# Gate and value products of the first network's second half by a seven-product scheme, and half of the second network's weights converted during its first pass

## The chip, the cores and the metric

One NeuronCore of a Trainium2 chip runs the whole program. The metric is the device time of one execution in microseconds (us). The kernel before takes 980.09 us (median of 3 runs, 979.85 to 980.98).

Engines: TensorE (PE, matmuls; its weight loads are PEld), VectorE (DVE), ScalarE (ACT), GpSimd (POOL) and SyncE (SP, which issues nearly all transfers).

## The reference, cut to what matters

Attention over 4 x 8 heads of 576 tokens gives x with 2304 tokens of 512 features. Two feed-forward networks follow:

```python
g = x @ w_gate                      # 512 -> 1536
silu = g * (1.0 / (1.0 + np.exp(-g)))
x = (silu * (x @ w_val)) @ w_out    # 1536 -> 512
h = np.maximum(x @ w_in, 0.0)       # 512 -> 2048
out = h * h @ w_out2                # 2048 -> 512
```

## The kernel before

**Precision.** The weights arrive as 64-bit words and are turned into 32-bit floats on the chip (`bit_stages`, L275: one ScalarE and three VectorE steps on a tile of 128 x 512). Then every operand, weight or activation, is split into a high part (a ScalarE copy, L323, L908, L993) and a low part (a VectorE subtraction, L326, L912, L996). Each product of two operands is three matmuls: high by high, high by low, low by high (`three`, L937 to L940).

**Stages.** Attention comes first, interleaved with the first half of the first network ("B1": 6 chunks of 128 hidden features, then "R" for the tiles that left some out). At about 264 us the attention is done and its buffers are released (`late`, L1181). The second half, "B2" (L1193 to L1204), runs 9 token tiles of 256 tokens over the chunks 6 to 11. Then the second network, "C", runs over 8 weight groups (each two chunks of 128) in two passes.

**A unit of B1 and B2** (`unit_tasks`, L960) is one tile and one chunk: 12 matmuls for the gate, 12 for the value, then tanh (ACT, L974), two VectorE steps (L982, L987), high and low (L993, L996), and 12 matmuls down into banks that collect the output. After a tile's last chunk `add_tasks` (L1055) adds the first half's output, read back into a "ys" buffer, and stores the sum.

**A unit of C** (`c_unit`) is a pair of tiles and a weight group. The four blocks of the up product (two halves of the features, two chunks, two tiles) are made by seven products of 6 matmuls instead of eight, in the order P1, P6, P5, P7, P2, P3, P4; VectorE and ScalarE add the products up between them (L1522, L1525, L1565). The operands are seven blocks or differences of blocks per pair (`x_pair`, L1358), in the "xs" buffers; the ninth tile runs alone with four products (`x_single`, L1438). The weights of a group need four combinations on VectorE (`up_task`, L1209, L1239). The first pass runs groups 0 to 3 for pairs 0, 1, 2 and the single tile, then pair 3 runs all eight, then groups 4 to 7 for the rest.

**Weights.** Converted tiles lie in "wg" slots: 18 from the start and 13 more once the attention's buffers are released (`NAMED`, L37). B1's 18 tiles leave theirs as the last tile of B1 uses them (`w_free`). All of C's 8 groups are converted during B2 (L1330 to L1336): groups 2 to 7 are stored to DRAM (`put_by`, L1300) and fetched again later (`fetch`, L1313), groups 0 and 1 stay. Raw weights pass through 4 "wst" buffers and 5 "wf" buffers.

**Order of the work.** The program's order on each engine is made by a list planner (`Order`, L121) that gives every stage a cost (`dve`, `act`, `products`, `dma`) and buffers it must take; units go by a due number, weights by "LATE". Each engine then runs its list in order, waiting by semaphore for what it needs. The planner's costs for VectorE are

```python
    def dve(n, fast=False):
        return 0.067 + n / (1920 if fast else 960)
```

Of the kernel before, what the change touches and what calls it, by code (L numbers as in the profile page):

```python
# [36 lines left out]
NAMED = {"wg": (18, 13), "xs": (4, 5), "wst": (4, 0)}  # L37
N_WST = NAMED["wst"][0]
# [22 lines left out]
def attn_moe_kernel(ctx: ExitStack, tc: tile.TileContext, qT, kT, vw, vin, vp, qp, kp, qs, ks, vs, maskc, masks, identc, wB, wC, out):  # L61
# [60 lines left out]
    class Order:  # L122
        def __init__(self):
            self.flying = []
            self.queues = {k: [] for k in ("x", "qk", "sum", "rows", "v", "att", "w", "mlp", "other", "done", "put")}
            n = {"att": N_ATT, "y": N_Y, "gv": N_GV, "p": N_P, "pt": N_PT, "v": N_V, "xt": N_XT}
            n |= {"wf": N_WF, "sg": N_SG, "hh": N_HH, "ys": 1, "rr": 0, "rh": 0, "rl": 0, "yc": 0}
# [134 lines left out]
    pools = {"wg": [tc.alloc_tile_pool(name="wg1", bufs=1, side="right")], "xs": [com], "wst": [com]}  # L262

    def slot_tile(kind):
        i = order.got[kind].pop(0)
        pool = pools[kind][i >= NAMED[kind][0]]
        shape, dtype = {"wg": ([128, 2, 512], F32R), "xs": ([128, 2, 2, T1], F32R), "wst": ([128, 512, 2], I32)}[kind]
        return i, pool.tile(shape, dtype, tag=f"{kind}{i}", bufs=1, name=kind)
# [3 lines left out]
    def w_give(*keys):  # L272
        return tuple(lambda key=key: ("wg", w_at[key]) for key in keys)
# [34 lines left out]
    def w_task(key, src, due, cond=None):  # L308
# [3 lines left out]
        def load():  # L312
            w_at[key], w_tiles[key] = slot_tile("wg")
            u["hi"], u["lo"] = (w_tiles[key][:, i] for i in range(2))
            u["at"], u["st"] = slot_tile("wst")
            nc.sync.dma_start(out=u["st"], in_=src)
# [5 lines left out]
        def high():  # L322
            nc.scalar.activation(out=u["hi"], in_=u["f"].bitcast(F32), func=AF.Copy)  # L323

        def low():
# [35 lines left out]
    def pool_rows(b, which, half, h):  # L361
        src, dst = (k_t, kd_t) if which == "k" else (q_t, qd_t)
        if b not in dst:

            room = com.tile([128, KD, T1], F32, tag="ys", name="ys").rearrange("p k n -> p (k n)")
# [304 lines left out]
    def global_tasks(b, ins, due, combos, end=False):  # L670
# [5 lines left out]
        def scores():  # L676
# [16 lines left out]
            [Stage("t", cost, scores, ("att", "att", "p", "p"), ("ys",) if end else (), lambda: after(ins + [consts]), 0.92)],  # L693
# [361 lines left out]
    def add_tasks(key, c0, n, dst, y_free):  # L1055
# [3 lines left out]
        def load():  # L1059
            u["y"] = com.tile([128, KD, T1], F32, tag="ys", name="ys")  # L1060
# [14 lines left out]
        def finish(cond, due):  # L1075
# [7 lines left out]
            y_out[key] = Task(adds + [Stage("d", dma(128 * 4 * n), store, (), ("ys",))], due, True)  # L1083
# [25 lines left out]
    def b1_finish(t, tags):  # L1109
# [3 lines left out]
        def make(cond, due):  # L1113
            u = {}

            def copy(i):
                if i == 0:
                    u["y"] = com.tile([128, KD, T1], F32, tag="ys", name="ys")
# [10 lines left out]
            stages.append(Stage("d", dma(128 * 4 * n), store, (), ("ys",)))  # L1129
# [50 lines left out]

    def late():  # L1181
        att.release()
        post = tc.alloc_tile_pool(name="post", bufs=1)
        at = after(sum(att_tasks.values(), sum(x_parts, [])))
        for kind, n in NAMED.items():
            pools[kind].append(post)
# [9 lines left out]
    ya = ("att", "att")  # L1196
# [8 lines left out]
    NFP = NF2 // 4  # L1205
    y2_sp = dram.tile([NTOK // 128, 128, DM], F32, name="y2_sp")
    out_t = out.rearrange("(r p) d -> r p d", p=128)

    def up_task(q, due):  # L1209
# [4 lines left out]
        def load(i):  # L1214
            if i == 0:
                for k in keys:
                    w_at[k], w_tiles[k] = slot_tile("wg")
            u["at", i], u["st", i] = slot_tile("wst")
            for k in (i, i + 2):
                u["f", k] = com.tile([128, 512], I32, tag="wf", bufs=N_WF, name="wf")  # L1220
            nc.sync.dma_start(out=u["st", i], in_=wC[2 * q + i][:, 0])

        def tile_half(i, c):
            return lambda: u["f", i].bitcast(F32)[:, c * 256 : c * 256 + 256]

        def both(k, src, n=512):
            def high():
                nc.scalar.activation(out=w_tiles[keys[k]][:, 0, :n], in_=src()[:, :n], func=AF.Copy)

            def low():  # L1230
                w = w_tiles[keys[k]]
                nc.vector.tensor_tensor(
                    out=w[:, 1, :n], in0=src()[:, :n], in1=w[:, 0, :n].bitcast(F32), op=ALU.subtract
                )

            return high, low

        def combine(o, a, b, op):
            return lambda: nc.vector.tensor_tensor(out=o(), in0=a(), in1=b(), op=op)  # L1239

        def read(i):
            return bit_stages(lambda: u["st", i], lambda: u["f", i], (), lambda: ("wst", u["at", i]))

        a11, a12, a21, a22 = (tile_half(i, c) for i in range(2) for c in range(2))
        s2, s3, s4 = tile_half(2, 0), tile_half(2, 1), tile_half(3, 0)
        high0, low0 = both(0, lambda: u["f", 0].bitcast(F32))
        high1, low1 = both(1, lambda: u["f", 1].bitcast(F32))
        high2, low2 = both(2, lambda: u["f", 2].bitcast(F32))
        high3, low3 = both(3, lambda: u["f", 3].bitcast(F32), 256)
        d = dma(128 * 1024)  # L1250
        second = Task([Stage("d", d, lambda: load(1), ("wst", "wf", "wf"))] + read(1), due, lead=W_LEAD)
        first = Task(
            [Stage("d", d, lambda: load(0), ("wst", "wf", "wf") + ("wg",) * 4, cond=lambda: after([late_]))]
            + read(0)
            + [
                Stage("a", act(512), high0),
                Stage("v", dve(512), low0),
                Stage("v", dve(256), combine(s3, a11, a21, ALU.subtract), cond=lambda: after([second])),
                Stage("v", dve(256), combine(a21, a21, a22, ALU.add)),
                Stage("v", dve(256), combine(s2, a21, a11, ALU.subtract)),  # L1260
                Stage("v", dve(256), combine(s4, a12, s2, ALU.subtract), (), ("wf",)),
                Stage("a", act(512), high1),
                Stage("v", dve(512), low1, (), ("wf",)),
                Stage("a", act(512), high2),
                Stage("v", dve(512), low2, (), ("wf",)),
                Stage("a", act(256), high3),
                Stage("v", dve(256), low3, (), ("wf",)),
            ],
            due,
            lead=W_LEAD,  # L1270
        )
        queues["w"] += [first, second]
        for k in keys:
            w_tasks[k] = first

    kept = {"rr": 2, "rh": 2, "rl": 2, "yc": 2}
    homes = {}

    def keep():
        slots = [(kind, i) for kind in ("wst", "wg") for i in order.got[kind]]  # L1280
        for kind in ("wst", "wg"):
            order.got[kind].clear()
        for kind, n in kept.items():
            homes[kind] = [slots.pop() for _ in range(n)]
            order.free[kind] = [0.0] * n

    def block_tile(name):
        kind, i = homes[name][0]
        homes[name].append(homes[name].pop(0))
        dtype = F32R if name in ("rh", "rl") else F32  # L1290
        pool = pools[kind][i >= NAMED[kind][0]]
        t = pool.tile([128, 2, 512], dtype, tag=f"{kind}{i}", bufs=1, name=name)
        return t if name == "yc" else t.rearrange("p b (c n) -> p (b c) n", c=2)

    w_sp = dram.tile([2 * NFP, 6, 128, 2, 512], F32, name="w_sp")

    def half_of(key):
        return 256 if key[0] == "U" and key[2] == 3 else 512

    def put_by(keys, task):  # L1300
        out_ = []
        for n, key in enumerate(keys):
            at = key[1], (4 + key[2] if key[0] == "D" else key[2])

            def store(key=key, at=at):
                n = half_of(key)
                nc.sync.dma_start(out=w_sp[at][:, :, :n], in_=w_tiles[key][:, :, :n].bitcast(F32))

            out_.append(Task([Stage("d", dma(128 * 1024), store, (), w_give(key), lambda: after([task]))], LATE))
            stored[key] = out_[-1]  # L1310
        queues["put"] += out_

    def fetch(key):  # L1313
# [535 lines left out]
```

## Time and profile before

| | us |
|---|---|
| median of 3 runs | 980.09 |
| the profiled execution | 980.34 |
| its span on the core | 978.6 |
| PE / PEld busy | 968.0 / 907.4 |
| VectorE / ScalarE busy | 668.2 / 385.3 |

The span is the time from the first to the last instruction on the core. Busy time is the union of an engine's records; matmul records are longer than their spacing, since matmuls are pipelined and their ends are modelled, so the spacing is read from their starts. The granted clock ("PEclk") is that of TensorE as a share of 2.4 GHz.

### The profile page before, as it was taken

The numbers are of one execution on the slowest core, as the hardware profiler recorded it, in microseconds if no ns is written. First come the engines' busy times: TensorE is split into PE (matmuls) and PEld (weight loads), VectorE is DVE, ScalarE is ACT, GpSimd is POOL, SyncE is SP. The second block draws the span as 40 slices with busy tenths as digits, with TensorE's granted clock in tenths as the row PEclk, the third lists the DMA queues.
The fourth block names the chain that finished last, engine by engine and source line by source line (L and its number), as shares of the span: only waits on it lengthen the run. The fifth ranks groups of instructions, "written<-read, shape, count | busy, mean of one in ns | idle before, by whom it ended". The sixth has DMA issues, their size and how long they took to land.

```text
span 978.6 us, 20467 instructions
## 1 busy us (share of the span) xinstructions
PE 968.0 (99%) x8397; PEld 907.4 (93%) x8397; DVE 668.2 (68%) x1500; ACT 385.3 (39%) x926; POOL 24.2 (2%) x31
## 2 busy tenths in 40 slices
PE   9989999999999999999999999999999999999998
PEld 7878999999999999999999999889889889898897
DVE  6998978469589488888898346647455437584643
ACT  4576464354455355454444222324233113232221
POOL 0202011000000000000000000000000000000000
PEclk9998999999999999999999999999999999999999
DMA  9989868051565257877892264113024802140202
GB/s 289 280 264 218 228 156 187 12 160 43 164 216 172 72 174 246 266 257 269 288 302 76 66 237 151 44 44 108 1 86 140 280 12 79 51 130 22 87 1 86
DMA packets 90874, 145.93 MB, mean 149 GB/s; under 512 B 21149, under 2 KB 60061, under 8 KB 90781
## 3 DMA queue, kind: packets, MB, share of 16 engines
q1 hardware_dynamic: 87324, 136.66, 42.6%
q0 software_dynamic: 3456, 7.96, 4.8%
q8 instruction: 66, 1.08, 0.4%
q14 instruction: 28, 0.22, 0.1%
HBM read 103.71 MB, written 40.89 MB: 148 GB/s over the span
## 4 chain that ended last, share of the span: by engine, by line
PE 97%; DVE 1%; ACT 1%; issue 0%; DVEq 0%; ACTq 0%
PE gv L938 14%; PE gv L940 13%; PE gv L939 13%; PE y L938 7%; PE y L940 7%; PE y L939 7%; PE att L1634 7%; PE att L1635 7%; PE att L1636 7%; PE att L542 2%; PE att L600 2%; PE y L1143 2%; PE att L690 2%; PE att L939 2%; PE att L938 1%; PE att L940 1%
## 5 line engine op out<-in xcount | busy, mean ns | idle before, releaser
L938 PE MATMUL gv<-xs,wg 128*128 128x256 f32 x1120 | 318.0, 284 | 0.0
L939 PE MATMUL gv<-xs,wg 128*128 128x256 f32 x1120 | 314.9, 281 | 0.0
L940 PE MATMUL gv<-xs,wg 128*128 128x256 f32 x1120 | 314.9, 281 | 0.0
L938 PEld LDWEIGHTS gv<-xs,wg 128*128 128x128 f32 x1120 | 212.3, 190 | 3.3 <-DVE sg L987 0.2
L939 PEld LDWEIGHTS gv<-xs,wg 128*128 128x128 f32 x1120 | 212.4, 190 | 2.0
L940 PEld LDWEIGHTS gv<-xs,wg 128*128 128x128 f32 x1120 | 212.3, 190 | 0.0
L1634 PE MATMUL att<-wg,rh 128*128 128x512 f32 x288 | 113.7, 395 | 0.0
L1635 PE MATMUL att<-wg,rh 128*128 128x512 f32 x288 | 113.5, 394 | 0.0
L1636 PE MATMUL att<-wg,rl 128*128 128x512 f32 x288 | 113.2, 393 | 0.0
L1525 DVE TENSOR_TENSOR rr<-y,ss 128x256 f32<-128x256 f32 x96 | 40.4, 421 | 94.2 <-PE y L940 94.1
L993 ACT ACTIVATE hh<-sg 128x256 fp32r<-128x256 f32 x108 | 44.8, 415 | 118.0 <-DVE sg L987 113.5
L938 PE MATMUL y<-hh,wg 128*128 128x256 f32 x312 | 90.9, 291 | 0.0
L1606 ACT ACTIVATE rh<-rr 128x512 fp32r<-128x512 f32 (+1 forms) x80 | 46.8, 588 | 108.0 <-DVE rr L1599 107.5
L939 PE MATMUL y<-hh,wg 128*128 128x256 f32 x312 | 88.6, 284 | 0.0
L940 PE MATMUL y<-hh,wg 128*128 128x256 f32 x312 | 88.5, 284 | 0.0
L987 DVE SCALAR_TENSOR_TENSOR sg<-sg,gv 128x256 f32<-128x256 f32 x108 | 45.2, 418 | 56.7 <-PE gv L940 55.5
L982 DVE SCALAR_TENSOR_TENSOR sg<-sg,gv 128x256 f32<-128x256 f32 x108 | 45.1, 418 | 39.6 <-ACT sg L974 39.2
L940 PE MATMUL y<-xs,wg 128*128 128x256 f32 x256 | 72.0, 281 | 0.0
L939 PE MATMUL y<-xs,wg 128*128 128x256 f32 x256 | 71.9, 281 | 0.0
L938 PE MATMUL y<-xs,wg 128*128 128x256 f32 x256 | 71.9, 281 | 0.0
L974 ACT ACTIVATE sg<-gv 128x256 f32<-128x256 f32 x108 | 41.4, 384 | 74.1 <-PE gv L940 71.7
L1636 PEld LDWEIGHTS att<-wg,rl 128*128 128x128 f32 x288 | 54.1, 188 | 12.8 <-DVE rl L1609 0.2
(110 smaller groups left out, 1762.3 us busy)
## 6 DMA issues: line engine op xcount, KB each, us to landing
wst<-wB SPq DMA_DIRECT2D x36, 512.0 KB, 6.8
wst<-wC SPq DMA_DIRECT2D x32, 512.0 KB, 5.9
w_sp<-wg SPq DMA_DIRECT2D x30, 512.0 KB, 10.0
wg<-w_sp SPq DMA_DIRECT2D x30, 512.0 KB, 4.7
y_sp<-ys SPq DMA_DIRECT2D x20, 512.0 KB, 3.5
xt<-y_sp SPq DMA_DIRECT2D x16, 512.0 KB, 3.8
xt<-x_sp SPq DMA_DIRECT2D x11, 512.0 KB, 4.7
ys<-y_sp SPq DMA_DIRECT2D x11, 512.0 KB, 4.7
```

The costliest lines, as they stand in the source:

```text
L938: nc.tensor.matmul(o, w[:, 0], x[:, 0], start=start, stop=False, skip_group_check=more)
L939: nc.tensor.matmul(o, w[:, 0], x[:, 1], start=False, stop=False, skip_group_check=more)
L940: nc.tensor.matmul(o, w[:, 1], x[:, 0], start=False, stop=stop, skip_group_check=more)
L974: nc.scalar.activation(out=u["s"], in_=u["g"][:, :n], func=AF.Tanh, scale=0.5)
L982: nc.vector.scalar_tensor_tensor(out=u["s"], in0=u["s"], scalar=1.0, in1=u["g"][:, :n], op0=ALU.add, op1=ALU.mult)
L987: nc.vector.scalar_tensor_tensor(out=u["s"], in0=u["s"], scalar=0.5, in1=u["v"][:, :n], op0=ALU.mult, op1=ALU.mult)
L993: nc.scalar.activation(out=u["h"][:, 0], in_=u["s"], func=AF.Copy)
L1525: return lambda: nc.vector.tensor_tensor(out=o(), in0=u[ps][:, :T1], in1=a(), op=ALU.add)
L1606: nc.scalar.activation(out=u["h"][:, b0:b1], in_=r(b0, b1), func=AF.Copy)
L1634: nc.tensor.matmul(o, h[:, c], w[:, 0], start=first and i == 0, stop=False)
L1635: nc.tensor.matmul(o, h[:, c], w[:, 1], start=False, stop=False)
L1636: nc.tensor.matmul(o, l[:, c], w[:, 0], start=False, stop=last and i == 1)
```

## The change

B2 is done by pairs of tiles, like C: the gate chunk and the value chunk take the place of the two chunks of a group, so seven products of 6 matmuls give gate and value of both tiles. The tiles are visited as pair 0, the ninth tile alone (four products), pairs 1, 2, 3. VectorE adds the products up (five additions and one ScalarE copy in a unit), then each tile has the steps tanh, silu, times, high, low and its down product as before, with sums in new "ss" and "h2" buffers. The gate and value weights of a chunk go through `up_task` and leave three "wg" tiles and one half-size "wh" tile. There are 6 extra "wg" slots instead of 13, and 6 "wh" slots; a tile takes its slot only when its high part is made, not when its raw data are loaded. When the first network's weights are done, two "wst" buffers become one more "wg" slot and a second "ys" buffer. Of C's groups, 2 and 3, then 0 and 1, are converted during B2; groups 4 to 7 are converted and stored during C's first pass, two "wg" slots then serving as raw buffers. Each converted tile is stored as soon as it is ready, where a group's four up tiles were stored together.

The diff, cut to its core:

```diff
-NAMED = {"wg": (18, 13), "xs": (4, 5), "wst": (4, 0)}
+NAMED = {"wg": (18, 6), "wh": (0, 6), "xs": (4, 5), "wst": (4, 0), "ss": (0, 8), "h2": (0, 4), "ys": (1, 0)}
...
-                Stage("d", dma(128 * 1024), load, ("wst", "wg"), cond=cond),
+                Stage("d", dma(128 * 1024), load, ("wst",) + ("wg",) * early, cond=cond),
...
-                Stage("a", act(512), high),
+                Stage("a", act(512), high, ("wg",) * (not early)),
...
-    for j in range(NF, NF1):
-        for i in range(3):
-            w_task((j, i), wB[j][:, i], LATE, lambda: after([late_]))
...
-    for t in range(NT1):
-        x_task(("B2", t), T1, lambda t=t: load_x(x_sp, t), lambda t=t: after([spills[t]]), ("xt",))
-        tags = ya if t % 2 == 0 else y2
-        early, finish = add_tasks(("B2", t), t * T1, T1, y_sp, tags)
-        for j in range(NF, NF1):
-            unit_tasks("B2", t, j, T1, j == NF, j == NF1 - 1, tags, finish, t == NT1 - 1, early)
...
+        put(0, 0, 512, ())
+        stages.append(combine(s3, a11, a21, ALU.subtract, ("wf",), lambda: after([second])))
+        stages.append(combine(a21, a21, a22, ALU.add))
+        put(1, 1, 512, ())
+        stages.append(combine(a11, a21, a11, ALU.subtract))
+        stages.append(combine(a12, a12, a11, ALU.subtract))
+        stages[-1].give = ("wf",)
+        put(2, 0, 512, ("wf",))
+        put(3, 2, 256, ("wf",))
...
+    for j in range(NF, NF1):
+        convert(("f", j), [wB[j][:, i] for i in range(2)], {(j, 2): wB[j][:, 2]})
+
+    def spare():
+        a, b = order.got["wst"]
+        order.got["wst"].clear()
+        alias["wg", SPARE_WG], alias["ys", 1] = ("wst", a), ("wst", b)
+        order.named["wg"].append((0.0, SPARE_WG))
+        order.named["ys"].append((0.0, 1))
...
+    def b2_unit(g, j, spent):
...
+            pe("P1", "x1", "A11", "B11", True, True, ("gv",))
+            pe("P6", "x2", "S2", "T2", True, True, ("gv",))
+            pe("P5", "z", "S1", "T1", True, True, ("y",))
+            pe("P7", "y", "S3", "T3", True, True, ("y",))
+            pe("P2", "x1", "A12", "B21", False, True, (), [lambda: at(mid, 0)()])
+            pe("P3", "z", "S4", "B22", False, True, (), [lambda: at(mid, 2)()])
+            pe("P4", "y", "A22", "T4", False, True, (), [lambda: at(mid, 3)()])
+            mid = Task(
+                [
+                    Stage("a", act(T1, True), begin, ("ss",), (), lambda: after([steps["P1"]])),
+                    Stage("v", d, add("s", "x2", "s"), (), ("gv",), lambda: after([steps["P6"]])),
+                    Stage("v", d, add("r", "z", "s", True), ("ss",), (), lambda: after([steps["P5"]])),
+                    Stage("v", d, add("r", "y", "r"), (), (), lambda: after([steps["P7"]])),
+                    Stage("v", d, add("g", "z", "s", True), ("ss",), ("y",), lambda: after([steps["P3"]])),
+                    Stage("v", d, add("s", "y", "s"), (), ("y",), lambda: after([steps["P4"]])),
+                ],
+                due - 1.5,
+                True,
+            )
...
+    visits = [0, NPAIRS, *range(1, NPAIRS)]
+    for g in visits:
+        whole = [spills[t] for t in range(2 * g, min(2 * g + 2, NT1))]
+        (x_single if g == NPAIRS else x_pair)(("B2", g), g, n_unit[0] + 0.5, x_sp, whole)
+        for j in range(NF, NF1):
+            b2_unit(g, j, g == visits[-1])
...
-    for q in range(KEEP_AT, 2 * NFP):
-        convert(q)
-        put_by([("U", q, i) for i in range(4)], w_tasks["U", q, 0])
-        for i in range(2):
-            put_by([("D", q, i)], w_tasks["D", q, i])
-    for q in range(KEEP_AT):
-        convert(q)
...
+    for q in range(KEEP_AT, NFP):
+        convert_c(q)
+        put_by(keys_of(q))
+    for q in range(KEEP_AT):
+        convert_c(q)
...
+    for q in range(KEEP_AT, NFP):
+        for key in keys_of(q):
+            fetch(key)
+    queues["w"].append(Task([Stage(None, 0.0, raw, ("wg",) * 2, cond=lambda: after([keep_b_]))], LATE))
+    for q in range(NFP, 2 * NFP):
+        convert_c(q)
+        put_by(keys_of(q))
+    for q in range(NFP, 2 * NFP):
+        for key in keys_of(q):
+            fetch(key)
```

## Rows read from the trace of the kernel before

**Rows 1.** The page: span, and busy time of each engine, share and instructions.
```profile
span 978.6 us, 20467 instructions
PE 968.0 (99%) x8397; PEld 907.4 (93%) x8397; DVE 668.2 (68%) x1500; ACT 385.3 (39%) x926; POOL 24.2 (2%) x31
```

**Rows 2.** Waits of PE, whole span: line, releaser, total us, times, longest us.
```profile
PE y L1143 <- ACT zeros L1137: 2.3, 1, 2.3
PE att L709 <- DVE xt L618: 1.2, 1, 1.2
...
PE att L600 <- ACT p L459: 0.2, 1, 0.2
```

**Rows 3.** The page: the chain that ended last, by engine.
```profile
PE 97%; DVE 1%; ACT 1%; issue 0%; DVEq 0%; ACTq 0%
```

**Rows 4.** Timeline of SP: output stores of B1's and B2's last tiles, first pass's last.
```profile
364.14 0.56 SPq L1123 DMA_DIRECT2D y_sp<-ys  x1
...
594.71 0.56 SPq L1068 DMA_DIRECT2D y_sp<-ys  x1
...
743.57 0.36 SPq L1703 DMA_DIRECT2D y_sp<-yc  x1
```

**Rows 5.** Timeline of PE in B2: first and last of 67 matmuls in a row.
```profile
364.00 0.28 PE L938 MATMUL att<-hh,wg 128*128 128x256 f32 x1
...
371.92 0.28 PE L938 MATMUL gv<-xs,wg 128*128 128x256 f32 x1
```

**Rows 6.** Stretches: length, busy of PE, PEld, DVE, ACT, POOL; PEclk, DMA share, GB/s.
```profile
338.00:364.00 26.00, 26.00 (x224) 26.00 (x223) 21.75 (x46) 14.91 (x31) 0.00 (x0) 1.00 0.61 201
...
494.00:519.00 25.00, 25.00 (x212) 25.00 (x211) 23.25 (x50) 11.87 (x25) 0.00 (x0) 1.00 0.87 294
...
543.00:570.00 27.00, 27.00 (x229) 27.00 (x228) 9.68 (x23) 6.78 (x16) 0.00 (x0) 1.00 0.23 71
...
364.00:595.00 231.00, 231.00 (x1936) 230.66 (x1935) 174.51 (x377) 93.86 (x204) 0.00 (x0) 1.00 0.64 219
```

**Rows 7.** Timeline of PE in C: first of 24 products, and the one after them.
```profile
850.09 0.28 PE L938 MATMUL y<-xs,wg 128*128 128x256 f32 x1
...
852.94 0.28 PE L938 MATMUL y<-xs,wg 128*128 128x256 f32 x1
```

**Rows 8.** Timeline of DVE in B2, operations back to back.
```profile
455.48 0.42 DVE L982 SCALAR_TENSOR_TENSOR sg<-sg,gv 128x256 f32<-128x256 f32 x1
455.81 0.69 DVE L297 SCALAR_TENSOR_TENSOR wf<-wst,wf 128x512 int32<-128x512 int32 x1
456.41 0.42 DVE L282 TENSOR_SCALAR wf<-wf 128x512 int32<-128x512 int32 x1
456.74 0.41 DVE L982 SCALAR_TENSOR_TENSOR sg<-sg,gv 128x256 f32<-128x256 f32 x1
```

**Rows 9.** Groups by form: busy us, mean ns | idle before.
```profile
L1525 DVE TENSOR_TENSOR rr<-y,ss 128x256 f32<-128x256 f32 x96 | 40.4, 421 | 94.2 <-PE y L940 94.1
...
L1232 DVE TENSOR_TENSOR wg<-wf,wg 128x512 fp32r<-128x512 f32 x24 | 16.4, 685 | 1.8 <-ACT wg L1228 1.8
...
L1228 ACT ACTIVATE wg<-wf 128x512 fp32r<-128x512 f32 x24 | 15.0, 624 | 9.2 <-DVE wf L297 9.2
...
L1239 DVE TENSOR_TENSOR wf<-wf 128x256 f32<-128x256 f32 x32 | 13.4, 420 | 0.1
...
L1565 ACT ACTIVATE ss<-gv 128x256 f32<-128x256 f32 x32 | 12.0, 374 | 25.2 <-PE gv L940 25.2
```

**Rows 10.** The page: stores of converted weights: count, KB each, median us to landing.
```profile
w_sp<-wg SPq DMA_DIRECT2D x30, 512.0 KB, 10.0
```

**Rows 11.** Stretches, columns as in rows 6: the start, and C's first pass.
```profile
0.00:100.00 100.00, 93.44 (x1201) 80.35 (x1203) 86.38 (x234) 59.78 (x180) 14.70 (x20) 0.95 0.94 263
...
600.00:650.00 50.00, 50.00 (x308) 44.67 (x307) 28.95 (x56) 14.21 (x28) 0.00 (x0) 1.00 0.20 70
```

More of the change, by code (lines that the diff above doesn't have):

```diff
@@ L1246, in up_task @@
[L1246 to L1249, printed above, removed]
-        d = dma(128 * 1024)
[L1251 to L1271, printed above, removed]
@@ L1272, in up_task @@
-        queues["w"] += [first, second]
[L1273 to L1311, printed above, removed]
@@ L1344, in attn_moe_kernel, with put @@
-    UP = {"A11": (0, 0), "A12": (0, 1), "S1": (1, 0), "A22": (1, 1), "S2": (2, 0), "S3": (2, 1), "S4": (3, 0)}
+        s3 = tile_half(2, 0)
+        d = dma(128 * 1024)
+        second = Task([Stage("d", d, lambda: load(1), ("wst",))] + read(1), due, lead=W_LEAD)
+        stages = [Stage("d", d, lambda: load(0), ("wst",), cond=lambda: after([late_]))] + read(0)
+        first = Task(stages, due, lead=W_LEAD)
+        def put(*args):
+            stages.extend(both(*args))
+            w_tasks[keys[args[0]]] = Part(first, len(stages) - 1)
@@ new lines, in attn_moe_kernel @@
+    for j in range(NF, NF1):
[6 more added lines that the diff above has]
+        order.named["ys"].append((0.0, 1))
+    SPARE_WG = sum(NAMED["wg"])
+    queues["w"].append(Task([Stage(None, 0.0, spare, ("wst",) * 2, cond=lambda: after([w_tasks[NF1 - 1, 2]]))], LATE))
@@ L1355, in attn_moe_kernel, with x_pair @@
     PROD = 6 * products(T1)
[L1358 to L1360 removed]
+    def x_pair(key, g, due, src, whole):
         u = {}
@@ L1478, in x_single, with make_pe, pe, go @@
         queues["done"].append(Task([Stage(None, 0.0, lambda: None, (), ("xt",), lambda: after(ends_))]))
+    ya = ("att", "att")
+    def make_pe(u, steps, key, q, due, single, last, free_x, spent):
+        def pe(name, ps, w, x, start, stop, take=(), cond=()):
+            def go():
+                if start:
+                    u[ps] = bank(take[0])
+                product(u[ps], factor(q, w), xh_t[key][x], start, stop, not (start or single))
+            before = list(steps.values())[-1:]
+            def ready():
+                if any(s.at == 0 for s in before):
+                    return None
+                needs = [f() for f in cond] + [after([x_tasks[key][x], w_tasks["U", q, UP[w][0]]])]
+                return None if None in needs else max(needs)
+            give = tuple(lambda x=x: ("xs", x_at[key][x]) for x in free_x.get(name, ()) if last)
+            if spent and name in ("P4", "Q4"):
+                give += w_give(*(("U", q, i) for i in range(4)))
+            steps[name] = Task([Stage("t", PROD, go, take, give, ready)], due + 0.01 * len(steps), True)
+        return pe
@@ new lines, in keys_of, with convert_c, keep_a @@
+    def keys_of(q):
+        return [("U", q, i) for i in range(4)] + [("D", q, i) for i in range(2)]
+    def convert_c(q):
+        convert(q, [wC[2 * q + i][:, 0] for i in range(2)], {("D", q, i): wC[2 * q + i][:, 1] for i in range(2)})
+    stored = {}
+    for q in range(KEEP_AT, NFP):
[3 more added lines that the diff above has]
+        convert_c(q)
+    def keep_a():
+        order.got["ss"].clear()
+        homes["rr"] = [("bk", 0), ("bk", 1)]
+        order.free["rr"] = [0.0] * 2
@@ new lines, in keep_b, with raw @@
+    def keep_b():
+        order.got["h2"].clear()
+        homes["rh"] = [("bk", 2), ("bk", 3)]
+        homes["rl"] = [("wst", i) for i in order.got["wst"]]
+        order.got["wst"].clear()
+        order.free["rh"], order.free["rl"] = [0.0] * 2, [0.0] * 2
+    def raw():
+        for n, i in enumerate(order.got["wg"]):
+            alias["wst", 10 + n] = "wg", i
+            order.named["wst"].append((0.0, 10 + n))
+        order.got["wg"].clear()
+    tails_, downs_b = b2_last
+    direct = [w_tasks[key] for q in range(KEEP_AT) for key in keys_of(q)]
@@ L1493, in c_unit @@
         prev = last_down[0]
-        def pe(name, ps, w, x, start, stop, take=(), cond=()):
-            def go():
-                if start:
-                    u[ps] = bank(take[0])
-                product(u[ps], factor(q, w), xh_t[key][x], start, stop, not (start or single))
-            before = list(steps.values())[-1:]
-            def ready():
-                if any(s.at == 0 for s in before):
-                    return None
-                needs = [f() for f in cond] + [after([x_tasks[key][x], w_tasks["U", q, UP[w][0]]])]
-                return None if None in needs else max(needs)
-            give = ((lambda: ("xs", x_at[key][x])),) * (last and free_x.get(name, False))
-            steps[name] = Task([Stage("t", PROD, go, take, give + w_free_of(name), ready)], due + 0.01 * len(steps), True)
-        def w_free_of(name):
-            return w_give(*(("U", q, i) for i in range(4))) if spent and name in ("P4", "Q4") else ()
+        pe = make_pe(u, steps, key, q, due, single, last, X_ONE if single else X_PAIR, spent)
         def start_r():
@@ L1584, in c_unit @@
             needs = [[at(mid, 4), at(one, 0)], [at(mid, 5)]]
-        if single:
-            steps["Q4"].stages[0].give += ((lambda: ("xs", x_at[key]["B11"])),) * last
-            steps["Q3"].stages[0].give = ()
         def tail(i):
@@ L1674, in c_begin @@
             yc_in[g, h] = Task(
-                [Stage("d", dma(128 * 1024), lambda h=h: load(h), ("yc",), (), lambda n=needs: after(n))], due, True
+                [Stage("d", dma(128 * 1024), lambda h=h: load(h), ("ys",), (), lambda n=needs: after(n))], due, True
             )
```

305 lines of the change are left out of this document (233 added, 72 removed).

## The prediction

> **What bounds the kernel now.** I read the busy table first: TensorE (PE) is busy for 968.0 of 978.6 us [rows 1]. The ends of matmuls are modelled, so a busy PE proves little, and the waits of PE come next: seven in the whole trace, 6.6 us together, the longest 2.3 and 1.2 us, all in the start or the attention lines [rows 2]. The chain that ended last agrees: PE 97% [rows 3]. So the end is set by the number of matmuls times their spacing.
>
> The spacing is read in the changed stage, the first network's second half (B2), from about 364 to 595 us [rows 4]. Matmuls of 256 columns start every 0.12 us without a gap: 66 intervals from 364.00 to 371.92 [rows 5]. Over the stage 1936 fall in 231 us, 0.1193 us each, at a granted clock of 1.00, the 2.4 GHz level [rows 6]. The second network (C) already runs the seven-product scheme: there 24 products start from 850.09 to 852.94, 0.1188 us each, without a gap too [rows 7]. The scheme itself need not starve PE.
>
> The second engine is VectorE (DVE): 23.3 of 25 us at its fullest in B2, 9.7 of 27 after 543 us [rows 6], where the conversion of C's weights has run out. Its records overlap, so I cost an operation from start to start: 0.335 us for 256 columns (455.48 to 455.81) and for the exponent step (456.41 to 456.74), 0.605 for 512 (455.81 to 456.41) [rows 8].
>
> **The matmuls removed.** B2 has 9 token tiles x 6 chunks x 36 matmuls = 1944 (12 gate, 12 value, 12 down). Afterwards a pair of tiles takes 7 products x 6 = 42 for gate and value where 48 stood, and 24 for down as before. Four pairs x 6 chunks are 24 units: 144 matmuls fewer. The ninth tile alone keeps 4 x 6 = 24 and saves nothing. 144 x 0.1193 = 17.2 us, all on PE, which sets the end. The 1008 products that pairs now take, at C's spacing instead of B2's, give 1008 x 0.0005 = 0.5 us more.
>
> [...] The rows show 118 to 120 ns in this stream, and the sum stays with them.
>
> **VectorE, added and moved.** (a) Five additions of products in each pair unit: 120 x 0.335 = 40.2 us. With the six operations of gate times value that both tiles had before, a pair unit needs 11 x 0.335 = 3.7 us beside 66 x 0.1193 = 7.9 us of PE. (b) Operand blocks: a pair needs 7 low parts and 4 differences of 512 columns, the single tile 3 and 1: 48 x 0.605 = 29.0 us where 18 x 0.605 = 10.9 stood, +18.1. (c) A chunk's gate and value weights take two raw reads of 0.335 + 2 x 0.605 = 1.545, four sums of 256 columns, low parts of 3 x 0.605 + 0.335: 6.58; with the down weight's 2.15 it is 8.73. Six chunks: 52.4 where 18 x 2.15 = 38.7 stood, +13.7. (d) A group of C's weights costs 6.58 + 2 x 2.15 = 10.9; four of eight leave B2 for C's first pass, -43.5. Net +28.5 us of VectorE in a stage that gets 17 shorter.
>
> [...]
>
> **Does VectorE still fit?** From the last tile of the first half (338 us) to the end of the new B2 (364 + 214 = 578) are 240 us. In it: that tile's own steps 6.0 + 1.2; B2's units 24 x 3.7 + 6 x 1.0 = 94.4; operand blocks of later visits 22.4, of C's first pair 6.7; nine output additions 10.9; four of C's groups 43.5; and what is left of B2's weights. These need slots: four "wg" per chunk, of which 6 spare ones exist instead of 13 until the last first-half tile frees the other 18. Before that, chunk 6 can run whole (8.7), chunk 7 but for three low parts (7.2), chunk 8's raw reads (3.1): 19.0; 33.4 are left. Sum 218.5, or 91% of 240. Before, PE saw no wait where VectorE was at 93% [rows 2, 6]. So I take the cover as enough on average, and look where it is thinnest.
>
> First pair, from 364 us: of the 33.4, 25.6 - 7.2 = 18.4 fit beside the last first-half tile; 15.0 remain, with 7.9 - 3.7 = 4.2 us per unit for them. The last chunk is due after five units, 39 us, in which 20.8 are free, less 2.4 for the single tile's blocks: it fits with 3 us over. Lower bound of the loss 0; upper, if nothing were converted beside that tile, 33.4 + 18.5 + 2.4 - 39.4 = 14.9 us. I take 0, because the trace shows this conversion running full beside that very tile (21.8 of 26 us) [rows 6].
>
> Entry of C: groups 0 and 1 find slots only as the last pair frees them. Some 5 us of them can run ahead, 16.8 stay for a visit of 47 us that needs 22.2 + 6.7 + 2.4 itself: 15.7 are free, and group 1 is due one C unit later. Groups 2 and 3 go through a single spare slot, 10 tiles x (0.62 high + 0.69 low + 10.0 landing of the store) = 113 us [rows 9, 10], in the 120 from 411 us (first pair done, and with it the first network's weights) to the last visit. Bounds 0 and the 1.1 us lacking plus one chain of high and low; I take 0, since group 1 has 10 us of grace.
>
> Changes of visit (four, and the entry of C): the next operand blocks follow one another out of slots that the last unit frees. C has such changes, with the same 9 slots, and no PE wait is listed there [rows 2]. Bounds 0, or one high and one low part each time, 5 x (0.62 + 0.69) = 6.6 us [rows 9]. I take 1.5, near the row without waits, for B2's last 24 down matmuls cover 2.8 us where C's, of 512 columns, cover twice that.
>
> C's first pass (595 to 744 us [rows 4]): VectorE was at 29 of 50 us [rows 11]; 43.5 more in 148 bring it to 87%, under the 93% above. The transfers that move along, 16 raw tiles and 22 tiles stored of 0.52 MB, 20 MB in all, raise the traffic from 70 to some 200 GB/s, below the 294 that B2 bore [rows 6, 11]. SP issues them in order, ahead of operand loads; what those lose is priced with the changes of visit. ScalarE gains 24 copies of 0.38 us, 13 highs of operands and 6 of weights, about 21 us on 94 of 231 [rows 6]: hidden; without that cover each copy stands between a first and a fifth product. Cost 0.
>
> **Sum.** The profiled execution took 980.3 us (span 978.6, 1.7 around it); the median of the runs is 0.2 lower. 980.3 - 17.2 - 0.5 + 1.5 = 964.1; against the median 963.9.
>
> **Rivals.** One: VectorE takes part of it back. If steps no longer overlap, because each waits for the one before, 0.42 and 0.69 take the place of 0.335 and 0.605 [rows 8], the 218.5 become about 260, 20 over the 240, of which C can take over 10.9: 9 lost, 973; with half of that slip, 968 to 969. For it: 91% load on one queue in order, where a late weight step can stand ahead of an addition that PE awaits. Against: full stretches kept 0.33 and 0.60 [rows 8].
>
> Two: nothing is won. In a unit the fifth to seventh products add to banks that ScalarE or VectorE must have read. If each pair unit waits 0.7 us, an addition and what it queues behind, 24 x 0.7 = 17: 981. Against: C runs the same order without gaps [rows 7].
>
> Three, slower: the first pair starves for weights. The buffers come free only as the last first-half tile ends its gate, value and down products, and raw data has five others; if that holds all 33.4 us of conversion back to 364, 14.9 are lost, near 979. The gaps, some 5 us ahead of each of three units, would then also cost clock: in the first 100 us, where PE has gaps (93.4 busy), 0.95 was granted, later 1.00 [rows 11]. Three units have 198 matmuls; half of them at the 1.2 GHz level are 99 x 0.119 = 11.8 us more: 991. It decides once over 18 us are lost there, which waits alone do not reach. Against: the conversion beside that tile in the trace [rows 6].
>
> That the change does not do what it says is a small chance within the second: seven products are what C already runs.
>
> **Chances.** PE stays the bound, 961 to 967: 0.64. VectorE takes part, 967 to 977: 0.20. Nothing won: 0.06. Starved first pair, slower: 0.10. About 0.2%, 2 us, can be told from no change. Faster 0.64 + 0.20 = 0.84, same 0.06, slower 0.10. The range, 961 to 974, takes in the first case and all of the second but its end: its low end is the sum without the 1.5, less 0.4 for the other 792 matmuls at C's spacing and 1 for the measurement, its high end rival one at full size.
>
> **What would show it.** Right: 8397 - 144 = 8253 matmuls; B2 ending near 578 us at 0.119 us a matmul; PE waits outside attention under 3 us; VectorE near nine tenths from 338 to 578 us and in C's first pass; C still 383 us long. Wrong: waits of PE's product lines for weight or operand lines of VectorE, most of all in the first pair, a granted clock under 1.00 there, or a spacing in B2 above 0.12 us.

## The result, and the profile after

The changed kernel takes 963.82 us (median of 4 runs, 963.13 to 965.32) beside 980.32 for the kernel before; ratio 0.9833, 95% interval 0.9816 to 0.985. Forecast were 963.9 us, range 961 to 974, and faster with a chance of 0.84.

The page of the changed kernel: span, busy time, and the chain that ended last, by engine (compare [rows 1, 3]).

```profile
span 963.5 us, 20487 instructions
PE 950.2 (99%) x8253; PEld 888.9 (92%) x8253; DVE 733.6 (76%) x1686; ACT 406.4 (42%) x975; POOL 23.9 (2%) x31
...
PE 92%; DVE 5%; ACT 1%; issue 1%; DMA 1%; SPq 0%; DVEq 0%; ACTq 0%
```

The 144 matmuls are gone (8397 to 8253). The chain now goes through VectorE for 5% of the span where it was 1%: PE still bounds the kernel, but VectorE has come close.

Its waits of PE: line, releaser, total us, times, longest us (compare [rows 2]). Those outside the start and attention are new.

```profile
PE att L1853 <- DVE rl L1826: 1.1, 1, 1.1
...
PE gv L975 <- DVE sg L1024: 0.6, 1, 0.6
...
PE gv L975 <- DVE ss L1564: 0.4, 1, 0.4
...
PE y L976 <- DVE hh L1033: 0.2, 1, 0.2
```

The timeline of SP after: output stores of a tile near the end of attention, of the last tile of the first half, of pair 0, of B2's last pair, and of the first pass's last tile (compare [rows 4]).

```profile
260.46 0.56 SPq L1161 DMA_DIRECT2D y_sp<-ys  x1
...
365.00 0.52 SPq L1161 DMA_DIRECT2D y_sp<-ys  x1
...
414.14 2.35 SPq L1105 DMA_DIRECT2D y_sp<-ys  x2
...
580.28 2.69 SPq L1105 DMA_DIRECT2D y_sp<-ys  x2
...
728.93 0.36 SPq L1928 DMA_DIRECT2D y_sp<-ys  x1
```

By these stores B2 lasts from 365.0 to 580.3, 215.3 us, where it took 594.7 - 364.1 = 230.6: 15.3 shorter. All before it ends 0.9 later, all after it takes 963.5 - 580.3 = 383.2 instead of 383.9. That makes the 15.1 us between the two spans; the profiled run of the changed kernel was the slowest of its four, so the medians differ by more, 16.5.

The stretches after, by visit (columns as in [rows 6]): the first half's last tile; pair 0; the single tile; pairs 1, 2, 3; the entry of C; and the whole from 338 to 578 us.

```profile
338.00:364.00 26.00, 25.22 (x210) 24.81 (x210) 25.68 (x57) 17.54 (x38) 0.00 (x0) 1.00 0.43 130
364.00:410.00 46.00, 45.60 (x385) 45.39 (x385) 45.34 (x113) 22.40 (x51) 0.00 (x0) 1.00 0.37 122
410.00:436.00 26.00, 26.00 (x222) 25.99 (x221) 21.94 (x46) 10.77 (x24) 0.00 (x0) 1.00 0.65 223
436.00:483.00 47.00, 47.00 (x400) 47.00 (x399) 41.18 (x101) 20.02 (x46) 0.00 (x0) 1.00 0.43 147
483.00:530.00 47.00, 47.00 (x400) 47.00 (x400) 37.56 (x90) 16.81 (x40) 0.00 (x0) 1.00 0.34 109
530.00:577.00 47.00, 47.00 (x400) 47.00 (x399) 46.11 (x112) 23.56 (x53) 0.00 (x0) 1.00 0.62 217
577.00:620.00 43.00, 41.87 (x278) 38.12 (x277) 40.12 (x81) 18.73 (x36) 0.00 (x0) 1.00 0.56 190
...
338.00:578.00 240.00, 238.82 (x2015) 238.20 (x2015) 218.82 (x516) 111.50 (x251) 0.00 (x0) 1.00 0.47 156
```

PE is idle for 26.00 - 25.22 = 0.8 us, then 0.4, then 43.00 - 41.87 = 1.1 at the entry of C: 2.3 in all, and for nothing between. VectorE is busy for 218.8 of 240 us, with 71.0 of 72 from 338 to 410 us and 46.1 of 47 in the last visit. These are the places to test.

### The profile page after: what moved, and what is told of

The parts are those of the page before. It is cut to its first block, busy times and chain, and to the rows that moved or that the text cites. A ratio compares the mean times of both kernels' runs of the same rounds, so it can differ in the third digit from the quotient of the medians.

```text
span 963.5 us, 20487 instructions
## 1 busy us (share of the span) xinstructions
PE 950.2 (99%) x8253; PEld 888.9 (92%) x8253; DVE 733.6 (76%) x1686; ACT 406.4 (42%) x975; POOL 23.9 (2%) x31
## 4 chain that ended last, share of the span: by engine, by line
PE 92%; DVE 5%; ACT 1%; issue 1%; DMA 1%; SPq 0%; DVEq 0%; ACTq 0%
PE gv L975 11%; PE gv L977 10%; PE gv L976 10%; PE y L975 8%; PE y L976 8%; PE y L977 8%; PE att L1851 7%; PE att L1853 7%; PE att L1852 7%; PE att L976 2%; PE att L977 2%; PE att L975 2%; PE att L579 2%; PE att L637 2%; PE att L727 2%; PE y L1181 1%
## 5 line engine op out<-in xcount | busy, mean ns | idle before, releaser
L975 PE MATMUL gv<-xs,wg 128*128 128x256 f32 x880 | 250.1, 284 | 1.0 <-DVE sg L1024 0.6
L977 PE MATMUL gv<-xs,wg 128*128 128x256 f32 x880 | 246.9, 281 | 0.0
L976 PE MATMUL gv<-xs,wg 128*128 128x256 f32 x880 | 246.8, 280 | 0.0
L975 PEld LDWEIGHTS gv<-xs,wg 128*128 128x128 f32 x880 | 166.0, 189 | 4.6 <-DVE sg L1024 1.0
L976 PEld LDWEIGHTS gv<-xs,wg 128*128 128x128 f32 x880 | 166.0, 189 | 1.9
L977 PEld LDWEIGHTS gv<-xs,wg 128*128 128x128 f32 x880 | 165.9, 189 | 0.0
L977 PE MATMUL y<-xs,wg 128*128 128x256 f32 x336 | 94.4, 281 | 0.0
L976 PE MATMUL y<-xs,wg 128*128 128x256 f32 x336 | 94.3, 281 | 0.0
L975 PE MATMUL y<-xs,wg 128*128 128x256 f32 x336 | 94.2, 280 | 0.0
L1816 DVE SCALAR_TENSOR_TENSOR rr<-rr 128x512 f32<-128x512 f32 (+1 forms) x80 | 50.0, 635 | 19.5 <-ACT rr L1745 17.8
L975 PEld LDWEIGHTS y<-xs,wg 128*128 128x128 f32 x336 | 63.5, 189 | 1.2
L976 PEld LDWEIGHTS y<-xs,wg 128*128 128x128 f32 x336 | 63.4, 189 | 1.2
L975 PE MATMUL y<-hh,wg 128*128 128x256 f32 x216 | 63.5, 294 | 0.0
L977 PEld LDWEIGHTS y<-xs,wg 128*128 128x128 f32 x336 | 63.5, 189 | 0.0
L1851 PEld LDWEIGHTS att<-wg,rh 128*128 128x128 f32 x288 | 54.2, 188 | 9.3 <-ACT rh L1823 0.4
L1852 PEld LDWEIGHTS att<-wg,rh 128*128 128x128 f32 x288 | 54.4, 189 | 8.9
```

The source lines that it names most:

```text
L975: nc.tensor.matmul(o, w[:, 0], x[:, 0], start=start, stop=False, skip_group_check=more)
L976: nc.tensor.matmul(o, w[:, 0], x[:, 1], start=False, stop=False, skip_group_check=more)
L977: nc.tensor.matmul(o, w[:, 1], x[:, 0], start=False, stop=stop, skip_group_check=more)
L1816: nc.vector.scalar_tensor_tensor(out=r(b0, b1), in0=r(b0, b1), scalar=0.0, in1=r(b0, b1), op0=ALU.max, op1=ALU.mult)
L1851: nc.tensor.matmul(o, h[:, c], w[:, 0], start=first and i == 0, stop=False)
L1852: nc.tensor.matmul(o, h[:, c], w[:, 1], start=False, stop=False)
```

## The experiments

The theory: the gain is the matmuls removed times their spacing; VectorE covers what was added, with a few us to spare in the first pair; and moving half of C's conversion earns nothing by itself but makes room. The rival: VectorE's queue paces the new B2, and PE only follows. Times below are compared with the changed kernel's 963.8; each was timed against the kernel before on its own chip.

The kernel before took 980.3 us beside the changed kernel, 981.2 and 980.4 in the two series of experiments, so a difference of medians can be off by about 1 us. The traces allow a closer comparison. The first 260 us, which no edit touches, differ by up to 2.3 us from trace to trace; the table leaves them out. It takes, from each timeline of SP, the output store near 260 us and the last one of C's first pass.

| kernel | store near 260 us | first pass's last store | between them | beside the changed kernel |
|---|---|---|---|---|
| before | 259.27 | 743.57 | 484.3 | +15.8 |
| changed | 260.46 | 728.93 | 468.5 | |
| eighth product | 260.64 | 750.56 | 489.9 | +21.5 |
| doubled, B2's weights | 259.24 | 739.06 | 479.8 | +11.3 |
| doubled, C's weights | 259.95 | 732.19 | 472.2 | +3.8 |
| doubled, late chunks | 259.55 | 733.46 | 473.9 | +5.4 |
| the same, planned | 260.58 | 735.99 | 475.4 | +6.9 |
| step left out | 258.35 | 725.84 | 467.5 | -1.0 |
| all converted early | 258.44 | 787.51 | 529.1 | +60.6 |

**An eighth product.** In `make_pe`, the first product of each pair unit of B2 twice, with its cost told to the planner:

```diff
+            n = 2 if name == "P1" and key[0] == "B2" else 1
...
-                product(u[ps], factor(q, w), xh_t[key][x], start, stop, not (start or single))
+                for _ in range(n):
+                    product(u[ps], factor(q, w), xh_t[key][x], start, stop, not (start or single))
...
-            steps[name] = Task([Stage("t", PROD, go, take, give, ready)], due + 0.01 * len(steps), True)
+            steps[name] = Task([Stage("t", n * PROD, go, take, give, ready)], due + 0.01 * len(steps), True)
```

> The changed kernel, with the first product P1 of every pair unit of B2 done twice: eight products in place of seven, the same result, no other step added. Theory (the number of matmuls times their spacing sets the gain, VectorE covers the rest): 144 x 0.1193 = 17.2 us come back, less up to 2 us of PE waits that the changed kernel has and that longer units hide: 979 to 981 us. Rival (VectorE's queue paces the new B2, PE only follows): longer units give VectorE room, less than 9 us come back, below 973 us.

Measured: 987.4 us (986.8 to 988.5), ratio to before 1.007 (1.0054 to 1.0085), span 985.1. The 144 matmuls come back and cost more than the theory had: 21.6 us of span, 23.6 of the medians. The entry of C in this kernel (columns as before):

```profile
577.00:620.00 43.00, 39.22 (x300) 37.06 (x299) 37.51 (x82) 17.11 (x38) 0.00 (x0) 1.00 0.65 233
```

PE is idle there for 3.8 us instead of 1.1, and for 2.1 from 338 to 410 us instead of 1.2: the planner, given longer units, made another order with 3.6 us more of waits. 17.2 + 3.6 = 20.8 of the 21.6. So the count of matmuls carries the gain, and the rival's bound of 973 is far off; but this kernel with eight products a pair is slower than the kernel before.

**VectorE work added, to B2's weights and to C's.** The sign step of the raw read is issued twice for chosen tiles; the order of everything else is as it was:

```diff
         def sign():
-            nc.vector.scalar_tensor_tensor(
-                out=f(), in0=st()[:, :, 1], scalar=-0x80000000, in1=f(), op0=ALU.bitwise_and, op1=ALU.bitwise_or
-            )
+            for _ in range(signs):
+                nc.vector.scalar_tensor_tensor(
+                    out=f(), in0=st()[:, :, 1], scalar=-0x80000000, in1=f(), op0=ALU.bitwise_and, op1=ALU.bitwise_or
+                )
```

For all of B2's chunks (`signs` is 2 where `isinstance(q, tuple) and q[1] >= NF1 // 2`):

> The changed kernel with the sign step of the conversion issued twice (the second changes nothing) for the 18 raw tiles of B2's own weights, in the same order of all other work. 10 of these steps lie after 338 us in the changed kernel's trace, 10 x 0.605 = 6 us of VectorE in a stretch where its records fill 71.0 of 72 us (338 to 410). Theory as predicted (some 3 us of slack in the first pair): about 3 us longer, 966 to 968. Rival one (no slack at all there, VectorE already paces the first pair): the whole 6 us, 969 to 971. Rival two (weights are ready long before their use): no change, within 1 us of 964.

For C's groups (2 where `not isinstance(q, tuple) and q < NF2 // 8`):

> The same doubling for the raw tiles of C's groups 0 to 3 alone, 16 x 0.605 = 9.7 us of VectorE spread from about 383 us to C's start. Theory: the visits of pairs 1 and 2 have room (VectorE 41.2 and 37.6 of 47 us), only the last visit and the entry of C (46.1 of 47) are tight: 0 to 3 us longer, 964 to 967. Rival (VectorE paces the whole of B2): all of it, 972 to 974.

The second edit does less than its expectation says. `NF2` is 16, so `NF2 // 8` is 2, and only groups 0 and 1 are doubled: 8 tiles, not 16. The count of sign steps shows it, in the changed kernel and in this one:

```profile
L323 DVE SCALAR_TENSOR_TENSOR wf<-wst,wf 128x512 int32<-128x512 int32 x68 | 46.5, 686 | 0.5
...
L324 DVE SCALAR_TENSOR_TENSOR wf<-wst,wf 128x512 int32<-128x512 int32 x76 | 51.9, 685 | 0.8
```

A doubled step also costs more than the 0.605 us of the expectations. The second issue reads what the first has just written. VectorE around one sign step, issued once (in the run with the late chunks below) and twice (here):

```profile
273.46 0.69 DVE L324 SCALAR_TENSOR_TENSOR wf<-wst,wf 128x512 int32<-128x512 int32 x1
274.06 0.42 DVE L1037 TENSOR_TENSOR hh<-sg,hh 128x256 fp32r<-128x256 f32 x1
...
273.26 1.42 DVE L324 SCALAR_TENSOR_TENSOR wf<-wst,wf 128x512 int32<-128x512 int32 x2
274.59 0.42 DVE L1037 TENSOR_TENSOR hh<-sg,hh 128x256 fp32r<-128x256 f32 x1
```

From the step's start to the next operation it is 0.60 us once and 1.33 twice, so an issue more costs 0.73. B2's 18 tiles get 13.1 us of VectorE instead of 10.9, groups 0 and 1 get 5.8.

Measured: 975.7 us (973.6 to 976.8; ratio 0.9945, 0.9932 to 0.9957) and 967.8 (966.9 to 968.6; ratio 0.9866, 0.9853 to 0.988). The first is beyond every expectation: 13.1 us of VectorE in all cost 11.9 by the medians, 11.3 by the table. The trace of that kernel says where. Three of its stores:

```profile
259.24 0.56 SPq L1165 DMA_DIRECT2D y_sp<-ys  x1
...
373.19 0.52 SPq L1165 DMA_DIRECT2D y_sp<-ys  x1
424.27 2.35 SPq L1109 DMA_DIRECT2D y_sp<-ys  x2
```

Counted from the first of them, 9.4 us are lost up to the last first-half tile (113.95 for 104.54) and 1.9 more up to pair 0's. Of the 9.4, 4.6 are lost already up to the tile before, whose store is at 343.31 where the changed kernel has 339.94. The waits of PE from 255 to 338 us and from 364 to 424, then PE's stretches around the longest wait (length, PE, clock, DMA, GB/s):

```profile
PE gv L979 <- DVE sg L1023: 0.9, 2, 0.7
PE y L980 <- DVE hh L1037: 0.8, 2, 0.4
PE gv L979 <- DVE sg L1028: 0.3, 1, 0.3
...
PE gv L979 <- DVE sg L1028: 2.2, 1, 2.2
PE gv L979 <- DVE ss L1568: 1.0, 1, 1.0
```
```profile
364.00:368.00 4.00, 2.56 (x22) 1.00 0.00 0
368.00:372.00 4.00, 3.24 (x15) 0.57 0.80 262
372.00:376.00 4.00, 4.00 (x36) 1.00 0.43 128
```

Before 338 us VectorE is busy for only 55 of 83 us, yet PE waits there for its gate steps: the conversion is packed, and from 290 to 300 us VectorE is busy for 9.9 of 10. After the 2.2 us wait the granted clock is 0.57 from 368 to 372 us, and from 369.13 to 371.49 us matmuls of 256 columns start 0.21 us apart: 3.24 busy us hold 15 matmuls where at 0.118 us they would hold 27, so the wait costs some 1.4 us once more.

The doubling of groups 0 and 1 costs 4.0 us by the medians, 3.8 by the table, of 5.8 added. Its steps stand from 468 us on, so it says nothing of the first pair. Three of them lie in the visits of pairs 1 and 2 and cost 0.8 us up to pair 2's store; the other five, in the last visit, where VectorE had 0.9 us of room, and behind it, cost 3.0 of their 3.7. The rival, that all of an added load is paid, is missed by 2 us only.

**Only the late chunks, without and with the planner told.** The doubling for chunks 9 to 11 alone, and the same with its cost in the stage:

```diff
-            Stage("v", dve(512), sign),
+            Stage("v", signs * dve(512), sign),
```

> The changed kernel with the sign step issued twice only for B2's chunks 9 to 11, in the planner's old order: 9 x 0.605 = 5.4 us of VectorE, all after the spare slots run out (from about 338 to 397 us). The doubling for all six chunks cost 11.9 us, for 10.9 us added. Theory (order fixed, no slack where conversion is packed, in the first pair least of all): nearly all is paid, and the clock falls where PE stands still over 2 us: 4.5 to 8 us longer, 968.5 to 972. Rival (most of the 11.9 came from chunks 6 to 8, whose conversion stands between the gate steps before 338 us): under 2.5 us longer, below 966.5.

> The same 9 x 0.605 = 5.4 us, but the planner is told of them, so that it orders all engines' work around them. Theory (the loss is one of capacity: VectorE is full from 338 to 410 us): within 1.5 us of the unplanned run. Rival (the loss is one of order: a step that the planner did not know of stands ahead of steps that PE awaits, while the prediction's 3 us of slack exist): under 2.5 us longer than the changed kernel, below 966.5.

Measured: 969.7 us (969.1 to 969.8; ratio 0.9876, 0.9861 to 0.9892) and 972.5 (969.6 to 974.0; ratio 0.9905, 0.9886 to 0.9925). The 9 steps are 6.6 us of VectorE. They cost 5.4 us by the table (5.9 by the medians, as its theory had it) where the order stayed, and 6.9 (8.7) where the planner made a new one, more than either of its expectations. PE from 338 us, in the first and then in the second:

```profile
338.00:364.00 26.00, 23.02 (x187) 22.03 (x185) 25.73 (x56) 14.98 (x33) 0.00 (x0) 1.00 0.36 107
364.00:410.00 46.00, 44.43 (x362) 43.23 (x363) 45.47 (x110) 21.64 (x48) 0.00 (x0) 1.00 0.40 132
...
338.00:364.00 26.00, 24.41 (x202) 23.80 (x200) 25.51 (x56) 17.00 (x36) 0.00 (x0) 1.00 0.39 122
364.00:410.00 46.00, 44.52 (x368) 43.72 (x369) 45.73 (x110) 20.45 (x46) 0.00 (x0) 1.00 0.32 101
```

In the first PE idles for 3.0 and 1.6 us there, VectorE stays full. The order that knows of the work loses less in the first pair, 3.6 us instead of 5.5 up to the single tile's store (counted from the store near 260 us), and most of the rest at the entry of C, where PE waits once for 2.9 us; the granted clock over the whole of this run is 0.993, in the changed kernel's profiled run 0.995. So in the order that the changed kernel runs some 1 us of the 6.6 is covered. An order made for the work covers 3.0 there, as much as the prediction had, and pays for it later. The loss is in part one of order, and that no order could do better is not shown.

**VectorE work taken away.** `signs` is 0 for B2's weights and for C's groups with `q < NF2 // 8`, again groups 0 and 1 and not 0 to 3:

> The sign step left out for the raw tiles of B2's own weights and of C's groups 0 to 3 (signs of those weights are lost): 34 x 0.605 = 20.6 us less VectorE, the same order of all other work. Theory: PE gains only what it waits in the changed kernel outside attention, 0.6 + 0.2 + 0.4 + 1.1 = 2.3 us: 961.5 to 963. Rival (VectorE paces B2): 5 us or more, below 959.

The trace has 42 sign steps for 68, so 26 x 0.605 = 15.7 us are taken away and not 20.6.

```profile
L324 DVE SCALAR_TENSOR_TENSOR wf<-wst,wf 128x512 int32<-128x512 int32 x42 | 28.6, 685 | 0.4
```

Measured: 963.5 us (962.2 to 964.4; ratio 0.9822, 0.9809 to 0.9835), span 960.4: no gain that the runs can tell from none; by the table 1.0 us. Both are below the 5 us of the rival. The whole stretch in this kernel:

```profile
338.00:578.00 240.00, 239.05 (x2020) 238.44 (x2019) 210.28 (x500) 109.14 (x246) 0.00 (x0) 1.00 0.47 156
```

VectorE is busy for 8.5 us less there and PE idles for 1.0 us instead of 1.2, and the 1.1 at the entry of C stays as well. What remains of waits hardly follows the load. The one at the entry of C is a place in VectorE's queue, as the changed kernel's trace shows (ScalarE first, then VectorE):

```profile
587.69 1.23 ACT L1823 ACTIVATE rh<-rr 128x512 fp32r<-128x512 f32 x2 [0.19 <-DVE rr L1816]
...
588.17 0.68 DVE L1367 TENSOR_TENSOR xs<-tr,xs 128x512 fp32r<-128x512 f32 x1
588.78 0.68 DVE L1353 TENSOR_TENSOR tr<-xt,tr 128x512 f32<-128x512 f32 x1
589.38 0.68 DVE L363 TENSOR_TENSOR wg<-wf,wg 128x512 fp32r<-128x512 f32 x1
589.98 1.89 DVE L1826 TENSOR_TENSOR rl<-rr,rh 128x512 fp32r<-128x512 f32 x3
```

The high parts `rh` are done by 588.92 at the latest, but the low parts `rl`, for which PE waits, start at 589.98 behind three steps for later operands and weights. The rival falls: at the load that the change has, taking VectorE work away does not make PE faster, so VectorE's load does not pace it.

**The second part, by itself and undone.** First the kernel before, without the three raw-read steps of some of C's groups. The condition is once more `q < NF2 // 8`, so these are groups 2 to 7 and not 4 to 7:

```diff
         def sign():
+            if not real:
+                return
...
-            return bit_stages(lambda: u["st", i], lambda: u["f", i], (), lambda: ("wst", u["at", i]))
+            return bit_stages(lambda: u["st", i], lambda: u["f", i], (), lambda: ("wst", u["at", i]), q < NF2 // 8)
```

> The kernel before, in the same order, with the three VectorE steps of the raw reads left out for C's groups 4 to 7 (their weights are then not the reference's): 16 x 1.545 = 24.7 us less VectorE in B2, as the second part of the change takes conversion out of B2, and nothing added to C's first pass. Theory (PE's matmuls alone set the end): no change, within 1 us of 980. Rival (the relief of VectorE in B2 is itself part of the gain): 2 us or more shorter, below 978.5.

Then the changed kernel with all of C's groups converted in B2:

```diff
-    for q in range(KEEP_AT, NFP):
+    for q in range(KEEP_AT, 2 * NFP):
         convert_c(q)
         put_by(keys_of(q))
...
-    for q in range(NFP, 2 * NFP):
-        convert_c(q)
-        put_by(keys_of(q))
```

> The changed kernel with the second part undone: groups 2 to 7 all converted and stored in B2, none in C's first pass. Theory: 43.5 us more VectorE in 240 us that hold 218 already, about 22 us too much, and the up weights of each further group keep a raw buffer until the last visit frees a half-size slot; PE waits at the entry of C: 985 to 1010 us, nothing lost before the last visit but a few us. Rival (the share of weights converted in C's pass does not matter, VectorE has room in B2 as it had before): within 3 us of 964.

Measured: 980.5 us (979.1 to 981.5; ratio 0.9996, 0.9985 to 1.0006) and 1024.3 (1024.2 to 1024.8; ratio 1.0435, 1.0415 to 1.0455). The first leaves out the steps of 24 tiles, 24 x 1.545 = 37.1 us, and VectorE's busy time falls from 668.2 to 633.2: taking even that much out of the old B2 changes nothing. Undoing the move costs 60 us, at the entry of C; the waits of PE from 530 us, the visits of pairs 1 and 2 and the entry of C, in that kernel:

```profile
PE gv L975 <- ACT wg L1259: 49.0, 4, 33.0
PE att L975 <- ACT h L1571: 2.1, 1, 2.1
```
```profile
436.00:483.00 47.00, 47.00 (x401) 47.00 (x400) 41.16 (x99) 19.78 (x45) 0.00 (x0) 1.00 0.44 150
483.00:530.00 47.00, 47.00 (x400) 47.00 (x399) 41.55 (x98) 19.05 (x44) 0.00 (x0) 1.00 0.50 170
...
577.00:620.00 43.00, 3.63 (x14) 2.81 (x13) 32.99 (x62) 13.87 (x24) 0.00 (x0) 0.54 0.79 280
```

C's first products stand before group 0's weights, which are converted last, and PE stands still for 39 of 43 us while VectorE and the transfers work through the backlog; the clock is at 0.54. 60 us is beyond the 21 to 46 of the theory. VectorE's time alone does not explain it: VectorE stands idle for 11.3 us in the visits of pairs 1 and 2, and for 10.0 of those 43 us, with conversion left to do. That the slots, which free up only in the last visit, held the conversion back would explain this; it was not tried apart.

## Why the prediction was right

**The matmuls.** 144 fewer, as counted; by the table the changed stages are 15.8 us shorter beside 17.2 + 0.5 - 1.5 = 16.2 forecast. The eighth product gave the reverse, 17.2 us and a worse order. The first term stands, and it carries the gain.

**VectorE's load.** The forecast for 338 to 578 us was 218.5 us of work; the profile has 218.8. The prices of 0.335 and 0.605 from start to start, and the list of what is added and moved, held. So did the 8253 matmuls, the end of B2 (580.3 for 578), C's 383 us, and the load in C's first pass, 87%:

```profile
580.00:729.00 149.00, 147.87 (x927) 132.75 (x926) 130.19 (x257) 67.61 (x132) 0.00 (x0) 1.00 0.54 188
```

Its fullest stretch is 95% (40.1 of 42 us from 620 to 662), still without a wait of PE after the entry.

**The loss of 1.5 us: near in size, wrong in place.** The step that failed is the one on the changes of visit, which priced the operand blocks at the four changes and at the entry of C. PE waits for no operand block at any of them. It loses 1.2 us in the last first-half tile and in pair 0, where I took 0, and 1.1 at the entry of C, for the low parts of C's own hidden features, which no term has. Together 2.3; that this is near the 1.5 is luck.

**The slack of 3 us in the first pair was not there in the order that runs.** This is the step that would have misled on a change only a little larger: 6.6 us of work more cost 5.4. I had set the free time of a stretch against the work left in it, as if all of it could be used. The trace shows VectorE full from 338 to 410 us with waits of PE already in it. The bound of 14.9 us for this place was the better guide to its risk.

**The rivals.** Rival one (VectorE takes part of it back) did not occur beyond the 2.3 us, but 6.6 us more of VectorE in the first pair bring it about. Rival two (a wait in each unit) is excluded by 47.00 of 47 us of PE in each of three visits. Rival three's mechanism, waits in the first pair and then the clock, is what the steps doubled for all of B2's chunks produced, at 0.57 of the clock; in the changed kernel itself the clock stays at 1.00 throughout B2. The lower level that this rival counts with stands in the trace of the kernel before, from 73 to 79.6 us (columns as in [rows 6]; then the first and last of 12 matmuls of 256 columns in a row):

```profile
73.00:79.60 6.60, 6.04 (x56) 5.40 (x55) 6.22 (x14) 3.16 (x10) 0.92 (x2) 0.50 0.96 217
```
```profile
76.91 0.41 PE L939 MATMUL y<-hh,wg 128*128 128x256 f32 x1
...
79.25 0.41 PE L938 MATMUL gv<-xs,wg 128*128 128x256 f32 x1
```

At 0.50 of the clock their 11 intervals take 2.34 us, 0.213 us each or 1.2 columns a ns; in proportion 1.00 would be 2.4, an estimate, where the stream in B2 starts 256 columns every 0.119 us, 2.15 a ns. So a matmul costs 0.09 us more there, not the 0.119 that this rival counts, and its 99 matmuls 9 us, not 11.8.

**The two prices.** The spacing of matmuls held: 1816 in 214.6 busy us from 365 to 580 us after, 118 ns each beside the 119.3 of the first term. So did the 0.335 of the additions, which read a product's bank. Two of them in the changed kernel, each with another operation of 256 columns behind it, and a sum of weights between buffers:

```profile
455.99 0.42 DVE L1511 TENSOR_TENSOR ss<-y,ss 128x256 f32<-128x256 f32 x1
456.33 0.41 DVE L1270 TENSOR_TENSOR wf<-wf 128x256 f32<-128x256 f32 x1
456.66 0.42 DVE L1511 TENSOR_TENSOR ss<-y,ss 128x256 f32<-128x256 f32 x1
456.99 0.42 DVE L1564 SCALAR_TENSOR_TENSOR ss<-ss 128x256 f32<-128x256 f32 x1
```

The additions take 0.34 and 0.33 us from start to start, the sum 0.33.

## What to carry to other kernels

Where one engine is full and nothing waits, fewer instructions on it are worth their spacing, and the question is whether the next engine can carry what replaces them: list its work from start to start, stretch by stretch, and compare it with the time that the shortened stage will have. A stretch in which the second engine is at 98% has little slack, even if its average elsewhere leaves a tenth: here 15.7 us less of VectorE's work over B2 gained about 1, and 6.6 us more in such a stretch cost 5.4. A move of work that earns nothing alone may be what makes the other part possible; undoing it shows what it is worth there (60 us here), but not whether time on the engine or buffers were what lacked. And count the changed instructions in the trace of each experiment before reading its time: three of the edits here reached other tiles than was meant.

## What was not expected of the hardware

A VectorE step issued a second time, reading what the first issue wrote, cost 0.73 us more, where the step by itself, with an independent one behind it, takes 0.60 from start to start. So the doubled steps were dearer than the expectations took them to be.

A wait of PE can cost clock on top of its own length, and need not. After PE had stood still for 2.2 us the clock was granted at 0.57 from 368 to 372 us, which cost 1.4 us more. In the run with the late chunks alone a wait of the same length was followed by a clock of 1.00, against its expectation; PE's stretches after its end at 363.9 us there:

```profile
362.00:366.00 4.00, 1.89 (x13) 1.00 0.64 211
366.00:370.00 4.00, 4.00 (x36) 1.00 0.48 165
```

The two waits are equally long, and one costs clock, the other none. Of two others, the 2.9 us stand in the planned run, with 0.993 granted over its whole length, and the 2.5 us at the entry of C with the eighth product have 1.00 around them, from 577 to 620 us. What sets them apart was not tried.
